# Attention with mixed heads and a SiLU MLP: one maximum instruction for two groups, over two neighbouring PSUM banks

## The chip, the cores and the metric

The kernel runs on one core of one Trainium2 chip. The metric is the device time of one execution in microseconds (us); the median of several executions counts. Engines are called TensorE (PE in the rows, PEld for its weight loads), VectorE (DVE), ScalarE (ACT), GpSimd (POOL) and SyncE (SP, which issues most DMAs).

## What is computed

The attention mixes its 12 heads twice, before and after the softmax; the result goes through a two-layer MLP. All arrays are float32 (the MLP's weights arrive as float64 and are taken apart in the kernel).

```python
# q, k, v: (4, 12, 448, 64); w_pre, w_post: (12, 12)
scores = scale * np.matmul(q, k.transpose(0, 1, 3, 2))
scores = np.einsum('bhij,hg->bgij', scores, w_pre)
scores = scores - np.max(scores, axis=-1, keepdims=True)
attn = np.exp(scores)
attn = attn / (np.sum(attn, axis=-1, keepdims=True) + 1e-09)
attn = np.einsum('bhij,hg->bgij', attn, w_post)
x = np.matmul(attn, v)                # then (tokens 1792, 768)
h = x @ w_in                          # 768 x 2048
out = (h / (1 + np.exp(-h))) @ w_out  # 2048 x 768
```

## The kernel before

The attention is cut into 16 tiles, four to a batch entry, of 100 or 120 query rows each. Within a tile the work runs over **groups** of 10 query rows: 10 rows times 12 heads, padded to 128 partitions, with 448 key columns. Two neighbouring groups are a **pair**; there are 184 groups and 92 pairs. After that comes the MLP (the products of line 624), from about 425 us to the end, in which the change has no instruction.

A pair goes through these steps, and the instruction names below are those of the rows:

- `scores` (lines 339 to 353) computes the scores of a later tile head by head (`pqk`), evicts them to `st` on ScalarE and VectorE, and scatters them by DMA into the rows of `g`.
- `mix_pair` (line 399) is the first head mixing: four products per pair (`pp<-g,wpre`), eight instructions in the trace. They fill two PSUM banks, one for each group. All four are done at about the same time, since two run side by side.
- `top` (line 405) takes the negated maximum of one group's 448 columns into `nm`, on VectorE. A pair needs two such instructions, one behind the other.
- `exp` (line 409) is the exponential on ScalarE, `e<-pp,nm`, with the row sum read out behind it (ACTIVATION_READ_ACCUMULATOR). It reads the group's bank and its `nm`. The first group's exponential is issued in the even step `i`, the second's in the next, odd step; both read PSUM, so the banks are free only after both.
- `bound_sums` and `norm_pair` (lines 418 to 425) make the scaled second mixing weights `wr`.
- `mix_pair_again` (line 437) is the second mixing (`pa<-wr,e`, 64 products per pair), one pair of banks `pa` for all pairs; `put_pair` (line 446) evicts it to `at` on ScalarE, and the next pair's `pa` products wait for that.
- `values` (line 368) multiplies with `v` (`po`), evicted by ScalarE to `x` (line 375).

`LEAD` is 4: the first mixing, maximum and exponentials run two pairs ahead of the second mixing. The order on each engine is the order in which the loop from line 667 writes the instructions; engines run in order. In an even step the loop writes `mix_pair` of the new pair, ScalarE's and VectorE's left-over evictions, the two `top`, and the first `exp`. Beside it the conversion of the MLP's weights (lines 63 to 93, `cw` and `cg`) puts VectorE, ScalarE and GpSimd work between the steps.

PSUM has eight banks: four in pool `ps_m` (scores, transposes, `po`), two in `ps_a` (`pa`, one tile for the whole loop), and two in `ps_p`, two buffers of one bank that every pair takes anew for its two groups. So the first mixing of a pair needs both banks back from the pair before it. During the opening (lines 541 to 556) `ps_p` also serves scores and transposes. The pair of groups 2 and 3 alone takes its banks from `ps_m`.

Of the kernel before, what the change touches and what calls it, by code (L numbers as in the profile page):

```python
# [8 lines left out]
F32 = mybir.dt.float32  # L9
# [4 lines left out]
ALU = mybir.AluOpType  # L14
AX = mybir.AxisListType
PSUM = bass.MemoryType.PSUM
# [87 lines left out]
def talking_heads_then_silu_mlp(  # L104
# [11 lines left out]
    nc = tc.nc  # L116
    ctx.enter_context(tc.manual_schedule())
    B, H, S, D = q.shape
# [4 lines left out]
    GP = 128  # L123
# [41 lines left out]
    mixing = ctx.enter_context(ExitStack())  # L165
    early_p = ctx.enter_context(ExitStack())

    def pool(name, bufs, stack=ctx, **kw):
        return stack.enter_context(tc.tile_pool(name=name, bufs=bufs, **kw))
# [7 lines left out]
    ps_m = pool("ps_m", 4, late_ps, side="right", space=PSUM)  # L177
    e_p = pool("e", 4, mixing, side="right")
    sm = pool("sm", 4, mixing, side="right")
    g_ps = [pool(f"g{o}", 1, st, side="right") for o, st in ((1, mixing), (0, early_p))]  # L180
    ps_p = pool("ps_p", 2, mixing, space=PSUM)
    ps_a = pool("ps_a", 1, mixing, space=PSUM)
    nat = pool("nat", 2, early_p)
    k2_p = pool("k2", 6, early_p)
# [2 lines left out]
    def pair(p, tag, dtype=F32R):  # L187
        return p.tile([128, 2, S], dtype, name=tag, tag=tag)
# [2 lines left out]
    banks = [ps_m]  # L191

    pa = ps_a.tile([128, 2, 512], F32, name="pa", tag="pa")
    turns = []

    def bank(p, name):
        if p is ps_a:
            turns.append(name)
            return pa[:, len(turns) % 2]
        return p.tile([128, 512], F32, name=name, tag="bank")  # L200

    v_tiles = [v2_p.tile([KV, 4, NJ, D], F32, name="v4", tag="v4") for _ in range(4)]
# [61 lines left out]
    def prep_k(b, h):  # L264

        pt = bank(banks[0], "pt")
        kn = kns.pop((b, h))
        for j in range(NJ):
            nc.tensor.transpose(pt[:, j * JT:(j + 1) * JT], kn[:, j].rearrange("p h d -> p (h d)"), ident[:JT, :JT])  # L269

        kh, kl = ks[b, h] = [k2_p.tile([128, S], F32R, name=x, tag=x) for x in ("kh", "kl")]

        def take_high():
            nc.scalar.copy(out=kh, in_=pt[:, :S])

        def take_low():
            nc.vector.tensor_sub(out=kl, in0=pt[:, :S], in1=raw(kh))
        return [(take_high, take_low)]
# [101 lines left out]
    class Group:  # L380
# [12 lines left out]
        def mix_pair(self, other, pool):  # L393

            o, np, p = self.place()
            self.p, other.p = bank(pool, "pp"), bank(pool, "pp")
            for r, c in ((0, 0), (1, 1), (0, 1), (1, 0)):
                rows = slice(HP * r, HP * (r + 1))
                nc.tensor.matmul(  # L399
                    (self, other)[r].p[HP * c:HP * (c + 1), :S], lhsT=wpre[rows],  # L400
                    rhs=gs[self.n][rows, o // R + c * np + p, :], start=True, stop=True)

        def top(self):
            self.nm = sm.tile([GP, 1], F32, name="nm", tag="nm")
            nc.vector.tensor_reduce(out=self.nm, in_=self.p[:GP, :S], axis=AX.X, op=ALU.max, negate=True)  # L405

        def exp(self, sums):
            self.e = e_p.tile([GP, S], F32, name="e", tag="e", bufs=6)
# [52 lines left out]
    at = lambda i: groups[i] if 0 <= i < len(groups) else None  # L461
# [13 lines left out]
    for n in range(1, len(seq)):  # L475
        p0, p1 = first[n - 1], first[n]
        spread = (0, 0, 0, 0, 2, 2) if n == 1 else (-6, -5, -4, -2, -1, 0) if p1 - p0 == 12 else (-6, -5, -4, -3, -2, -1)
        for h in range(0 if n > 1 else 2 * NE, H, 2):
            i = p0 + spread[h // 2]
# [23 lines left out]
    n_last = first[len(seq) - 1]  # L503
# [55 lines left out]
    keep_busy(2)  # L559
    for i in range(0, LEAD, 2):  # L560
        at(i).mix_pair(at(i + 1), (ps_p, ps_m)[i // 2])
        for j in (i, i + 1):
            at(j).top()
        at(i).exp_first()
        at(i + 1).exp(at(i).s[:, 1:2])
        at(i).bound_sums((nc.vector, nc.gpsimd)[i // 2])
        if not i:
            at(0).norm_pair(at(1))
# [29 lines left out]
    def load_part(j):  # L598
        src, k, p = parts[j]
        if src is wo_dram:  # L600
            for _ in conv:
                pass
        raws[j] = box["w"].tile([128, 4, 128], F32R, name="wl", tag="wl", bufs=WB)
        nc.sync.dma_start(out=raw(raws[j]), in_=src[:, 4 * p:4 * p + 4, k])

    def ready_part(j):
        wl = raws.pop(j)
        wh = box["w"].tile([128, 4, 128], F32R, name="wh", tag="wh", bufs=WB)
        nc.scalar.copy(out=wh, in_=raw(wl))  # L609
        nc.gpsimd.tensor_sub(out=wl, in0=raw(wl), in1=raw(wh))  # L610
        ready[j] = wh, wl

    def product(s, p):

        kind, k, u, a = steps[s]
        nk = HC if kind == "i" else HF
        todo = []
        for n in range(nk):
            wh, wl = (x[:, (a * nk + n) % 4] for x in ready[part_of(kind, k, a * nk + n)])
            x = ops[u][n]  # L620
            todo += [(0, wh, x[:, 0]), (1, wh, x[:, 1]), (2, wl, x[:, 0])]
        todo.sort(key=lambda t: t[0])
        for n, (_, w, x) in enumerate(todo):
            nc.tensor.matmul(p[:, :T], lhsT=w, rhs=x, start=(n == 0), stop=(n == len(todo) - 1))  # L624

    def halve(src, dst):

        nc.scalar.copy(out=dst[:, 0], in_=src)
        yield
        nc.vector.tensor_sub(out=dst[:, 1], in0=src, in1=raw(dst[:, 0]))  # L630
# [36 lines left out]
    for i in range(len(groups) + 1):  # L667
        g, new, old = at(i), at(i + LEAD), at(i - 1)
        if i == n_last:
            early_p.close()  # L670
            xw = pool("xw", 1)
            box["w"] = pool("w", 1)

            ops[0] = [pair(xw, f"op0{c}") for c in range(HC)]
            splits = [halve(xs[0][0, 0, c], ops[0][c]) for c in range(HC)]
        for what, args in early[i]:
            what(*args)
        fresh = [new, at(i + LEAD + 1)] if new and i % 2 == 0 else []
        if fresh:
            new.mix_pair(fresh[1], ps_p)  # L680
        if i >= n_last:
            for x in fresh:
                x.top()
        if new and i % 2:
            new.exp(at(i + LEAD - 1).s[:, 1:2])
        for take, _ in done:
            take()
        if 0 < i < len(groups) and i % 2 == 0:
            at(i - 2).put_pair()
        for take, _ in later:  # L690
            if take:
                take()
        if i == len(groups) - 1:
            old.put_pair()
        if any(what is scores for what, _ in work[i]):
            for _, take in later:
                if take:
                    take()
            later = []
        if i < n_last:  # L700
            for x in fresh:
                x.top()
        for _, take in later:
            if take:
                take()
        if i % 2 and at(i + 3):
            at(i + 3).bound_sums()
        if i % 2 == 0 and at(i + 2):
            at(i + 2).norm_pair(at(i + 3))
        if scaled:  # L710
            next(conv)
            scaled = False
        for take in lows:
            take()
        if fresh:
            new.exp_first()
        later, done, highs, lows = [], [], [], []
        for what, args in sorted(work[i], key=lambda x: order.index(x[0])):
            while len(later) + len(done) + len(lows) + 1 + (what is scores) > 4:
                for take in (done or later).pop(0):  # L720
                    if take:
                        take()
            new_takes = what(*args) or []
            if what in (prep_q, prep_k):
                highs += [take for take, _ in new_takes]
                lows += [take for _, take in new_takes]
                new_takes = []
            if what is scores:
                while len(later) > 1:
                    for take in later.pop(0):  # L730
                        if take:
                            take()
            (done if what is values else later).extend(new_takes)
        for take in highs:
            take()
        if i == len(groups) - 2:
            phs.append(bank(ps_m, "ph"))
            product(0, phs[0])
        if g and i % 2 == 0:
            g.mix_pair_again(at(i + 1))  # L740
        if i == len(groups) - 2:
            phs.append(bank(ps_m, "ph"))
            product(1, phs[1])
        if i >= n_last:
            if i >= n_last + 2 and splits:
                if next(splits[0], 1):
                    splits.pop(0)
            if n_last + 2 <= i < n_last + 2 + WB:
                load_part(i - n_last - 2)
        if i in lighter:  # L750
            scaled = next(conv, None)
        if i in (len(groups) - 5, len(groups) - 3):
            ready_part(len(ready))
# [7 lines left out]
    for h in (0, HH):  # L761
        ready_part(len(ready))
        banks[:] = [(ps_m, ps_h)[h // HH]]
        new = values(len(seq) - 1, h // 2, HC)[0]
# [85 lines left out]
    for s, (kind, m, u, a) in enumerate(steps):  # L850
# [14 lines left out]
        p = None  # L865
        if s >= len(phs):
            p = bank(ps_h, "ph")
# [56 lines left out]
```

## Time and profile before

| what | us |
|---|---|
| three executions | 880.78, 886.57, 889.70 |
| their median | 886.57 |
| span of the profiled execution, first to last instruction | 869.5 |
| median less that span | 17.1 |

The profile is of one execution. Its page gives the span alone; what lies around the span is taken from the median, so it is 17.1 us, and 11.3 to 20.2 us by the single executions. Windows and rows give times from the span's start. An engine's busy time is the union of its instructions; a TensorE product that is held back in the middle of a series counts as busy until the series ends.

### The profile page before, as it was taken

The numbers are of one execution on the slowest core, as the hardware profiler recorded it, in microseconds if no ns is written. First come the engines' busy times: TensorE is split into PE (matmuls) and PEld (weight loads), VectorE is DVE, ScalarE is ACT, GpSimd is POOL, SyncE is SP. The second block draws the span as 40 slices with busy tenths as digits, with TensorE's granted clock in tenths as the row PEclk, the third lists the DMA queues.
The fourth block names the chain that finished last, engine by engine and source line by source line (L and its number), as shares of the span: only waits on it lengthen the run. The fifth ranks groups of instructions, "written<-read, shape, count | busy, mean of one in ns | idle before, by whom it ended". The sixth has DMA issues, their size and how long they took to land.

```text
span 869.5 us, 27489 instructions
## 1 busy us (share of the span) xinstructions
PE 825.0 (95%) x11058; PEld 654.1 (75%) x11058; DVE 622.9 (72%) x1218; ACT 526.6 (61%) x1178; POOL 404.4 (47%) x681
## 2 busy tenths in 40 slices
PE   8798999899998999898899999899999999999997
PEld 5355666567665666565799888789999989999886
DVE  5454777577766777666759989998878589983332
ACT  4576888688876878787665652325784346343342
POOL 6131545453645546355856675656642233233020
PEclk8999999999999999999999999999999999999999
DMA  7569778887798877864643553544221142012234
GB/s 148 169 188 207 207 210 242 221 230 211 228 237 220 241 198 216 215 196 139 193 133 125 162 180 104 145 148 140 92 74 49 35 115 81 29 49 73 75 84 106
DMA packets 162343, 132.89 MB, mean 153 GB/s; under 512 B 50409, under 2 KB 155861, under 8 KB 162215
## 3 DMA queue, kind: packets, MB, share of 16 engines
q1 hardware_dynamic: 158809, 129.39, 53.3%
q8 instruction: 87, 1.43, 0.7%
q0 software_dynamic: 544, 1.03, 0.5%
q10 hardware_dynamic: 2862, 0.71, 0.4%
q14 instruction: 41, 0.34, 0.1%
HBM read 64.01 MB, written 27.53 MB: 105 GB/s over the span
## 4 chain that ended last, share of the span: by engine, by line
PE 65%; DVE 15%; DMA 9%; ACT 4%; POOL 3%; issue 3%; SPq 2%; POOLq 0%; DVEq 0%; ACTq 0%
PE ph L624 35%; PE pa L437 8%; PE po L368 7%; PE pp L399 6%; PE pqk L339 6%; DMA g<-st 3%; DVE x L634 2%; DVE op L630 2%; DVE nm L405 2%; DMA qn<-in_q 2%; ACT e L409 2%; DVE cg L92 1%; DMA v<-in_v 1%; PE pt L269 1%; PE ptt L844 1%
## 5 line engine op out<-in xcount | busy, mean ns | idle before, releaser
L624 PE MATMUL ph<-op,wh 128*128 128x448 f32 x924 | 223.5, 370 | 3.7 <-DVE g L823 1.4
L610 POOL TENSOR_TENSOR wl<-wl,wh 128x512 fp32r<-128x512 f32 x84 | 121.3, 1461 | 154.4 <-ACT wh L609 152.0
L624 PEld LDWEIGHTS ph<-op,wh 128*128 128x128 f32 x924 | 172.6, 189 | 20.9 <-DVE g L823 2.7
L405 DVE TENSOR_REDUCE nm<-pp 128x1 f32<-128x448 f32 x184 | 106.1, 618 | 73.1 <-PE pp L399 72.8
L425 POOL TENSOR_SCALAR wr<-wpost,r 128x60 f32<-128x60 f32 x184 | 72.0, 404 | 172.4 <-DVE r L422 120.7
L409 ACT ACTIVATE e<-pp,nm 128x448 f32<-128x448 f32 x184 | 115.4, 631 | 47.9 <-DVE nm L405 45.3
L437 PEld LDWEIGHTS pa<-wr,e 64*64 64x64 f32 (+1 forms) x5888 | 96.0, 131 | 44.3 <-issue 25.8
L437 PE MATMUL pa<-wr,e 64*64 64x60 f32 (+1 forms) x5888 | 108.2, 218 | 14.0 <-ACT at L446 7.7
L624 PE MATMUL ph<-op,wl 128*128 128x448 f32 x462 | 119.6, 367 | 0.4 <-POOL wl L610 0.4
L399 PE MATMUL pp<-g,wpre 64*64 64x448 f32 x736 | 101.9, 573 | 10.8 <-ACT e L409 6.4
L66 POOL TENSOR_TENSOR cg<-cw,cg 128x256 f32<-128x256 f32 x96 | 74.0, 771 | 77.9 <-DVE cw L63 75.7
L624 PEld LDWEIGHTS ph<-op,wl 128*128 128x128 f32 x462 | 87.2, 189 | 7.7 <-POOL wl L610 0.7
L446 ACT COPY at<-pa 120x960 f32<-120x960 f32 x92 | 90.0, 978 | 3.3 <-PE pa L437 3.2
L368 PE MATMUL po<-at,v 120*64 120x120 f32 (+1 forms) x1536 | 87.3, 266 | 2.8 <-issue 2.1
L368 PEld LDWEIGHTS po<-at,v 120*64 120x64 f32 x1536 | 76.4, 138 | 15.2 <-issue 6.4
L90 ACT ACTIVATE cg<-cg,ebias 128x256 int32<-128x256 int32 x96 | 49.6, 516 | 50.8 <-DVE cg L86 49.6
L344 DVE COPY st<-pqk 120x448 f32<-120x448 f32 (+1 forms) x89 | 54.9, 617 | 32.6 <-PE pqk L339 16.8
L609 ACT CAST wh<-wl 128x512 fp32r<-128x512 f32 x84 | 50.9, 617 | 43.1 <-DMA wl<-wo_dram 28.0
L92 DVE SCALAR_TENSOR_TENSOR cg<-cw,cg 128x256 int32<-128x256 int32 x96 | 51.8, 540 | 25.0 <-ACT cg L90 24.7
L624 PE MATMUL ph<-x,wh 128*128 128x448 f32 x252 | 64.8, 365 | 0.0
L339 PEld LDWEIGHTS pqk<-kh,qh 64*120 64x120 f32 (+1 forms) x186 | 18.6, 175 | 43.1 <-issue 14.9
L399 PEld LDWEIGHTS pp<-g,wpre 64*64 64x64 f32 x736 | 23.0, 134 | 37.0 <-ACT e L409 15.5
(122 smaller groups left out, 1398.8 us busy)
## 6 DMA issues: line engine op xcount, KB each, us to landing
g<-st SPq DMA_DIRECT2D x132, 210.0 KB
cw<-in_moe_w_in SPq DMA_DIRECT2D x48, 256.0 KB
cw<-in_moe_w_out SPq DMA_DIRECT2D x48, 256.0 KB
wi_dram<-cg SPq DMA_DIRECT2D x24, 448.0 KB
wo_dram<-cg SPq DMA_DIRECT2D x24, 448.0 KB
wl<-wi_dram SPq DMA_DIRECT2D x42, 256.0 KB
wl<-wo_dram SPq DMA_DIRECT2D x42, 256.0 KB
g<-st SPq DMA_DIRECT2D x48, 175.0 KB
```

The costliest lines, as they stand in the source:

```text
L66: nc.gpsimd.tensor_mul(out=e, in0=m, in1=e)
L92: nc.vector.scalar_tensor_tensor(out=e, in0=hi, scalar=-2 ** 31, in1=e, op0=ALU.bitwise_and, op1=ALU.bitwise_or)
L339: nc.tensor.matmul(ps[i][:m, :S], lhsT=q_[rows, hh, :m], rhs=k_[rows], start=(step == 0), stop=(step == 2))
L368: nc.tensor.matmul(po[i * D:(i + 1) * D, c * m:(c + 1) * m], lhsT=vs[b, h][:, i, j, :], rhs=ats[n][:, j, h + i, :m], start=(j == 0), stop= ...
L399: nc.tensor.matmul((self, other)[r].p[HP * c:HP * (c + 1), :S], lhsT=wpre[rows], rhs=gs[self.n][rows, o // R + c * np + p, :], start=True, ...
L405: nc.vector.tensor_reduce(out=self.nm, in_=self.p[:GP, :S], axis=AX.X, op=ALU.max, negate=True)
L409: nc.scalar.activation(out=self.e, in_=self.p[:GP, :S], func=AF.Exp, bias=self.nm, scale=1.0, accum_out=sums)
L425: nc.gpsimd.tensor_scalar(out=g.wr, in0=wpost.rearrange("p g i -> p (g i)"), scalar1=r[:, i:i + 1], scalar2=1.0, op0=ALU.mult, op1=ALU.mult)
L437: nc.tensor.matmul(half[64 * c:64 * c + m, s, j * GH:(j + 1) * GH], lhsT=g.e[rows, j * JT + c * JH:j * JT + c * JH + m], rhs=g.wr[rows], s ...
L446: nc.scalar.copy(out=ats[self.n].rearrange("p j g t -> p (j g) t")[:, :, o:o + 2 * R].rearrange("p x (c i) -> p x c i", i=RH), in_=pa[:KV] ...
L610: nc.gpsimd.tensor_sub(out=wl, in0=raw(wl), in1=raw(wh))
L624: nc.tensor.matmul(p[:, :T], lhsT=w, rhs=x, start=(n == 0), stop=(n == len(todo) - 1))
```

## The change

The two one-bank buffers of `ps_p` become one tile `pp` of two neighbouring banks that lives through the whole loop; `bank` hands out its halves in turn during the opening. `top` of one group becomes `top_pair` of a pair: one `tensor_reduce` reads `[128, 2, 448]` over both banks and writes two columns of a new tile `nm` `[128, 2]`. The pair from `ps_m` keeps its two instructions. The place of the reductions in the loop is the same.

```diff
-    ps_p = pool("ps_p", 2, mixing, space=PSUM)
+    ps_p = pool("ps_p", 1, mixing, space=PSUM)
...
+    pp = ps_p.tile([128, 2, 512], F32, name="pp", tag="pp")
...
     def bank(p, name):
-        if p is ps_a:
-            turns.append(name)
-            return pa[:, len(turns) % 2]
+        if id(p) in turns:
+            turns[id(p)] += 1
+            return (pa if p is ps_a else pp)[:, turns[id(p)] % 2]
...
-            self.p, other.p = bank(pool, "pp"), bank(pool, "pp")
+            self.p, other.p = (pp[:, 0], pp[:, 1]) if pool is ps_p else (bank(pool, "pp"), bank(pool, "pp"))
...
-        def top(self):
-            self.nm = sm.tile([GP, 1], F32, name="nm", tag="nm")
-            nc.vector.tensor_reduce(out=self.nm, in_=self.p[:GP, :S], axis=AX.X, op=ALU.max, negate=True)
+        def top_pair(self, other, pool):
+            nm = sm.tile([GP, 2], F32, name="nm", tag="nm")
+            self.nm, other.nm = nm[:, 0:1], nm[:, 1:2]
+            if pool is ps_p:
+                nc.vector.tensor_reduce(out=nm, in_=pp[:, :, :S], axis=AX.X, op=ALU.max, negate=True)
+            else:
+                for g in (self, other):
+                    nc.vector.tensor_reduce(out=g.nm, in_=g.p[:GP, :S], axis=AX.X, op=ALU.max, negate=True)
...
-            for x in fresh:
-                x.top()
+        if fresh and i < n_last:
+            new.top_pair(fresh[1], ps_p)
```

On VectorE, in the middle of the loop, one pair's share of the queue before the change (the reductions are line 405; what stands behind them is the reciprocal of an earlier pair and an eviction):

```order
L93 TENSOR_SCALAR cw<-cw 128x256 [waits DVE_49]
L405 TENSOR_REDUCE nm<-pp 128x1 [waits PE_49] x2
L422 RECIPROCAL r<-r 128x2 [waits Pool_49]
L277 TENSOR_TENSOR kl<-pt,kh 128x448 [waits Activation_49]
L86 TENSOR_SCALAR cg<-cw 128x256 [waits DMAHW6_49]
```

The same place of the changed kernel, in which its lines have other numbers (408 is the new reduction):

```order
L93 TENSOR_SCALAR cw<-cw 128x256 [waits DVE_49]
L408 TENSOR_REDUCE nm<-pp 128x2 [waits PE_49]
L428 RECIPROCAL r<-r 128x2 [waits Pool_49]
L278 TENSOR_TENSOR kl<-pt,kh 128x448 [waits Activation_49]
L86 TENSOR_SCALAR cg<-cw 128x256 [waits DMAHW3_49]
```

Two reductions with one column of results each became one with two; the neighbours on the queue are the same.

On TensorE, the first mixing of a pair behind the products with `v`, before the change:

```order
L368 MATMUL po<-at,v_134 64x120 x15
L399 MATMUL pp<-g,wpre 64x448 [waits Activation_49]
L399 MATMUL pp<-g,wpre 64x448 [waits PE_49,Activation_49]
L399 MATMUL pp<-g,wpre 64x448 x2
L339 MATMUL pqk<-kh,qh 120x448 [waits DVE_49] x2
```

The same place of the changed kernel:

```order
L369 MATMUL po<-at,v_135 64x120 x15
L400 MATMUL pp<-g,wpre 64x448 [waits DVE_49,Activation_49]
L400 MATMUL pp<-g,wpre 64x448 x3
L340 MATMUL pqk<-kh,qh 120x448
L340 MATMUL pqk<-kh,qh 120x448 [waits DVE_49]
```

Before, the first product waits for ScalarE's reading of the first bank and the second product for that of the second bank; now the first product carries a wait on ScalarE and VectorE for the tile, and the other three carry none. On no engine does any other instruction change its place.

## Rows read from the trace of the kernel before

**Rows 1.** The page, parts 1 (engines' busy us) and 4 (the chain).
```profile
PE 825.0 (95%) x11058; PEld 654.1 (75%) x11058; DVE 622.9 (72%) x1218; ACT 526.6 (61%) x1178; POOL 404.4 (47%) x681
PE ph L624 35%; PE pa L437 8%; PE po L368 7%; PE pp L399 6%; PE pqk L339 6%; DMA g<-st 3%; DVE x L634 2%; DVE op L630 2%; DVE nm L405 2%; DMA qn<-in_q 2%; ACT e L409 2%; DVE cg L92 1%; DMA v<-in_v 1%; PE pt L269 1%; PE ptt L844 1%
```

**Rows 2.** Windows: length, busy us (instructions) of PE, PEld, DVE, ACT, POOL.
```profile
44.00:425.00 381.00, 357.34 (x8414) 239.07 (x8415) 262.87 (x628) 296.96 (x719) 189.03 (x442) 1.00 0.78 213
```

**Rows 3.** Lines, 0 to 560 us: busy us, mean ns, idle before.
```profile
L405 DVE TENSOR_REDUCE nm<-pp 128x1 f32<-128x448 f32 x184 | 106.1, 618 | 73.1 <-PE pp L399 72.8
L409 ACT ACTIVATE e<-pp,nm 128x448 f32<-128x448 f32 x184 | 115.4, 631 | 47.9 <-DVE nm L405 45.3 <-POOL cg L72 0.7 <-POOL cg L71 0.4
L422 DVE RECIPROCAL r<-r 128x2 f32<-128x2 f32 x92 | 14.4, 157 | 5.0 <-POOL r L418 4.7
L523 DVE MEMSET g<- 128x2688 f32 x1 | 2.3, 2298 | 0.5 <-issue 0.5
```

**Rows 4.** Timeline (start us, length us, instruction) of a pair with spare time.
```profile
121.64 0.98 PE L399 MATMUL pp<-g,wpre 64*64 64x448 f32 x8
122.68 1.16 DVE L405 TENSOR_REDUCE nm<-pp 128x1 f32<-128x448 f32 x2 [0.42 <-PE pp L399]
123.42 0.63 ACT L409 ACTIVATE e<-pp,nm 128x448 f32<-128x448 f32 x1
124.04 0.63 ACT L409 ACTIVATE e<-pp,nm 128x448 f32<-128x448 f32 x1
124.56 0.20 ACT L409 ACTIVATION_READ_ACCUMULATOR e<-pp,nm 128x1 f32 x1
125.25 0.98 PE L399 MATMUL pp<-g,wpre 64*64 64x448 f32 x8
```

**Rows 5.** Timeline, a pair whose products wait for the pair before.
```profile
408.42 1.59 PE L399 MATMUL pp<-g,wpre 64*64 64x448 f32 x8
408.78 0.20 ACT L409 ACTIVATION_READ_ACCUMULATOR e<-pp,nm 128x1 f32 x1
409.03 0.20 PEld L399 LDWEIGHTS pp<-g,wpre 64*64 64x64 f32 x6 [0.43 <-ACT e L409]
410.49 1.14 DVE L405 TENSOR_REDUCE nm<-pp 128x1 f32<-128x448 f32 x2
411.21 0.63 ACT L409 ACTIVATE e<-pp,nm 128x448 f32<-128x448 f32 x1 [0.99 <-DVE nm L405]
```

**Rows 6.** Line 409, 27 to 425 us, who waited for it: us, times.
```profile
  PEld pp L399: 15.5, 25
  PE pp L399: 6.4, 7
```

**Rows 7.** Waits, 44 to 425 us: us in total, times, longest.
```profile
DVE nm L405 <- PE pp L399: 66.3, 68, 4.2
ACT e L409 <- DVE nm L405: 36.1, 54, 2.2
PE pa L437 <- ACT at L446: 6.6, 14, 0.9
```

**Rows 8.** Timeline of TensorE alone, line 399.
```profile
27.92 4.84 PE L399 MATMUL pp<-g,wpre 64*64 64x448 f32 x24 [3.70 <-DMA g<-first]
52.26 1.42 PE L399 MATMUL pp<-g,wpre 64*64 64x448 f32 x8
...
411.99 1.59 PE L399 MATMUL pp<-g,wpre 64*64 64x448 f32 x8 [0.46 <-ACT e L409]
```

**Rows 9.** Timeline at two further places, ScalarE and what follows on TensorE.
```profile
217.97 0.98 ACT L446 COPY at<-pa 120x960 f32<-120x960 f32 x1
219.10 1.11 PE L437 MATMUL pa<-wr,e 64*64 64x60 f32 x63
...
289.89 0.21 ACT L409 ACTIVATION_READ_ACCUMULATOR e<-pp,nm 128x1 f32 x1
290.42 0.98 PE L399 MATMUL pp<-g,wpre 64*64 64x448 f32 x8
```

More of the change, by code (lines that the diff above doesn't have):

```diff
@@ L193, in talking_heads_then_silu_mlp @@
     pa = ps_a.tile([128, 2, 512], F32, name="pa", tag="pa")
-    turns = []
+    pp = ps_p.tile([128, 2, 512], F32, name="pp", tag="pp")
+    turns = {id(ps_a): 0, id(ps_p): 0}
     def bank(p, name):
-        if p is ps_a:
-            turns.append(name)
-            return pa[:, len(turns) % 2]
+        if id(p) in turns:
+            turns[id(p)] += 1
+            return (pa if p is ps_a else pp)[:, turns[id(p)] % 2]
         return p.tile([128, 512], F32, name=name, tag="bank")
@@ L561, in talking_heads_then_silu_mlp @@
         at(i).mix_pair(at(i + 1), (ps_p, ps_m)[i // 2])
-        for j in (i, i + 1):
-            at(j).top()
+        at(i).top_pair(at(i + 1), (ps_p, ps_m)[i // 2])
         at(i).exp_first()
@@ L680, in talking_heads_then_silu_mlp @@
             new.mix_pair(fresh[1], ps_p)
-        if i >= n_last:
-            for x in fresh:
-                x.top()
+        if fresh and i >= n_last:
+            new.top_pair(fresh[1], ps_p)
         if new and i % 2:
@@ L699, in talking_heads_then_silu_mlp @@
             later = []
-        if i < n_last:
-            for x in fresh:
-                x.top()
+        if fresh and i < n_last:
+            new.top_pair(fresh[1], ps_p)
         for _, take in later:
```

## The prediction

> **What bounds the kernel now.** I read the page first [rows 1]: TensorE is busy 95% of the span, and its lines hold 65% of the chain that ended last; the maximum (`nm`) and the exponential (`e`) hold 2% each. So the maximum matters only where TensorE waits for something behind it. The window of the mixing loop comes next [rows 2]: in its 381 us TensorE is busy 357, ScalarE 297 and VectorE 263. VectorE has 118 us to spare there, and 66 of them are waits of the maximum for the first mixing [rows 7]: VectorE isn't what holds the loop. Then the timeline of single pairs shows the ring that the change touches: mixing products, maximum, two exponentials, and back to the products of the next pair, which need both banks.
>
> In a usual pair [rows 4] the products start at 121.64 and the two reductions at 122.68. The first exponential starts at 123.42: 0.74 after the reductions start, 0.12 after the first has ended, while the second still runs. The second exponential starts at 124.04 and its sum is read out by 124.76. TensorE comes to the next pair's products at 125.25, 0.49 after that. Here TensorE had other work, and the ring has time to spare.
>
> In a tight pair [rows 5] the products start at 408.42 on the first bank, but the other weight loads wait until 409.03, which is 0.05 after the read-out of the second exponential (408.78 and 0.20). The series then lasts 1.59 instead of 0.98. There the ring sets the time. In all, 25 weight loads and 7 products waited for line 409 [rows 6]; the timeline of line 399 shows 14 pairs between 44 and 412 us, of which the first and last plain ones stand in [rows 8], that last 1.27 to 1.59 us, and two more start within 0.1 of the read-out. That makes 16 pairs with nothing to spare.
>
> **The change, part by part.**
>
> *The reduction itself.* One of today's takes 618 ns for 448 columns and the reciprocal, an instruction with 2 columns, 157 ns [rows 3]. The difference over 446 columns is 1.03 ns a column; 896 columns then take 157 + 894 x 1.03 = 1.08 us. No row has such an instruction, so it is bounded: above by two of today's with no overlap, 1.24 us; below by 618 ns and 448 columns at the rate of the long memset (2298 ns for 2688 columns, 0.86 ns each [rows 3]), 1.00 us. I take 1.08, from the same operation and memory.
>
> *VectorE's gain.* Two reductions take 1.16 us from start to end [rows 4], so 91 pairs free 91 x 0.08 = 7 us of VectorE (between -7 and 15 by the bounds). I cost this at 0 on the path: the cover is the 66 us that the maximum waits for TensorE anyway [rows 7]. Without the cover it is a gain of 7 us.
>
> The Trainium skill (Perfetto Trace Analysis, Optimizing Scalar/DVE Operations) puts the cost of an instruction's data access on VectorE from PSUM at about 125 ns; by that estimate 91 instructions fewer free 11 us instead of 7, still under the same cover. The same section says that grouping helps when the engine is saturated, and that breaking instructions up may let work end sooner when the engine is not saturated and makes others wait; the window with VectorE busy 263 of 381 us [rows 2] is of the second kind, and so the page speaks against this change.
>
> *The first exponential's start.* It was released at the end of the first reduction, 0.62 after the start, and will be at the end of the only one, 1.08: later by 0.46 us (0.38 to 0.62 by the bounds). The second exponential stands behind it on ScalarE's queue and moves as far. So do the evictions queued behind it (`st`, `at`, `x`, the casts), until ScalarE's next idle stretch takes the delay up. 54 of the first exponentials already waited for the maximum, 36.1 us in all [rows 7]; this should come to roughly 36 + 88 x 0.46 = 76 us.
>
> *What of it reaches TensorE.* I went through the pairs by the time from the read-out of the second exponential to the next products, less the 0.05 us that a release takes:
> - 16 pairs have none to spare: 16 x 0.46 = 7.4 us.
> - 4 pairs have 0.1 to 0.3; the tightest of a second kind is a pair with 0.32 from read-out to products (289.89 and 0.21, then 290.42 [rows 9]). They lose 0.37, 0.36, 0.19 and 0.17: 1.1 us.
> - 19 pairs are like the usual one, with 0.39 to 0.45 to spare [rows 4]: 0.04 each, 0.8 us.
> - The other 50 or so have more than 0.46: nothing.
> - The second mixing waits for the eviction of `pa` 14 times [rows 7]. In most of these ScalarE stood idle ahead of the eviction, for `po`, and takes the delay up there. In two pairs it has no such gap, as at 217.97: the eviction ends at 218.95 and `pa` starts at 219.10 [rows 9]. 2 x 0.45 = 0.9 us.
> - At the loop's opening three pairs' products stand in one series [rows 8]; the third needs the first's banks, so one more delay counts: 0.5 us.
>
> *The wait of the products.* The first product now waits for the whole tile, and before for its own bank. In a tight pair that gave nothing: after the second release at 409.03 the series took another 0.98 us [rows 5], as long as a whole one. Cost 0. If the early start was worth anything, it is at most the 0.61 between 408.42 and 409.03, in 16 pairs 10 us; I keep that for the upper end. What is queued behind the waiting product is TensorE's whole stream, which is why the delays above add up.
>
> The sum: 7.4 + 1.1 + 0.8 + 0.9 + 0.5 = 10.7 us. The profiled span becomes 880.2; with 17.1 around it, as the median has, 897.3 us, against 886.6 before. With a delay of 0.38 the sum is 8 us, with 0.62 it is 17 (16 x 0.62, 4 x 0.43, 19 x 0.2, 1.2 and 0.6).
>
> **The rivals.**
>
> *ScalarE becomes the bound.* ScalarE is idle 84 us in the window [rows 2], 36 of them for the maximum. Of the other 48 the change takes up to 40. Every eviction then comes later than TensorE wants it, and also the pairs with time to spare lose it. Against it: in the usual pair 0.49 us are spare. If half of the 88 x 0.46 reaches TensorE, it is 20 us: 907 us; if all, 40 us: 927.
>
> *It is hidden anyway.* TensorE stands idle 24 us in the window [rows 2] and waits at places that the ring doesn't set, for score scatters and loads. A pair that comes 0.46 later may meet a wait that would have held it all the same. Against it: those waits are fed by the same loop and move with it. Price 0 to 5 us; 889 us.
>
> *Faster.* VectorE's queue behind the maximum (evictions of scores, `cg` and `cw` of the weights) ends earlier by 0.08 us a pair; if that queue, not the exponential, is what TensorE waits for, the gain is 7 us: 879.5, and 15 us or 872 with a reduction of 1.00. It decides only where the maximum starts late because VectorE is behind, as at 410.49 [rows 5]; most starts are set by the products, 68 waits [rows 7]. Over 1% needs a reduction below about 1.06 us and no tight pair at all. The Trainium skill's rule on grouping, in the section named above, would give this if VectorE were saturated.
>
> **How the numbers follow.** The forecast above has a chance of 0.50, with a range of its own from 892 to 905. ScalarE as the bound has 0.17, hidden 0.25, faster 0.08. 1% is 8.9 us, about what a measurement of this kernel, whose runs lie 880.8 to 889.7, can tell from no change. Over 895.4 lie four fifths of the forecast (0.41) and the first rival (0.17): slower 0.58. The rest of the forecast and the hidden case make 0.35 for within 1%, and 0.07 is left for faster. The range from 886 to 911 leaves out the faster case (0.08), the upper half of the first rival (0.08) and the lowest part of the hidden one (about 0.04).
>
> **What the profile after would show.** The reductions: 91 instructions of about 1.08 us; over 1.2 or under 1.0 would make the first term wrong. First exponentials 1.2 us behind the start of the reduction instead of 0.74. ScalarE's waits for the maximum at about 76 us in the window instead of 36. Waits of line 399's loads for line 409 more often than 25 times, and stretched series in some 20 pairs or more. The time from 425 us to the end unchanged. If the loop's end moves by less than 5 us while these waits do appear, the hidden case is right; if it moves by 20, with `at`, `st` and `x` as new causes of TensorE's waits, ScalarE became the bound.

## The result, and the profile after

The changed kernel is slower by 1.28%.

| | before | after |
|---|---|---|
| median of 10 executions, us | 882.5 (874.7 to 889.7) | 891.2 (887.7 to 899.1) |
| ratio, 95% interval | | 1.0128 (1.0086 to 1.0171) |
| span of the profiled execution, us | 869.5 | 886.7 |
| from the last pair's mixing products to the end, us | 451.6 | 451.7 |

The profiled execution after took 888.4 us in all, 1.7 us more than its span. The last line of the table is the span less the end of the last products of line 399 (417.9 us) or of its counterpart, line 400 (435.0 us): behind the loop nothing changed, so all of the difference lies in the loop. The ratio is of undisturbed executions alone: the slowest of before, 889.7 us, lies 1.7% above the fastest and doesn't count in it, so it isn't the quotient of the two medians, 1.0098.

In the changed kernel the first mixing is line 400, the long maximum line 408, the exponential line 415, the reciprocal line 428. First the page's busy times and the window that answers to [rows 2]:

```profile
PE 822.7 (93%) x11058; PEld 653.9 (74%) x11058; DVE 614.4 (69%) x1127; ACT 526.6 (59%) x1178; POOL 403.0 (45%) x681
```

```profile
44.00:434.00 390.00, 351.66 (x8224) 235.16 (x8224) 247.95 (x527) 289.90 (x702) 180.99 (x429) 0.98 0.74 203
```

This window ends just ahead of the last mixing products (435.0 us), that of [rows 2] 7 us behind them (417.9 us), so only the shares compare. VectorE has 8.5 us less to do over the span (622.9 before [rows 1]), and the kernel is longer all the same. By lines, 0 to 560 us, as [rows 3]:

```profile
L415 ACT ACTIVATE e<-pp,nm 128x448 f32<-128x448 f32 x184 | 115.3, 630 | 79.7 <-DVE r L428 63.2 <-DVE nm L408 14.6 <-DVE nm L411 1.0
L408 DVE TENSOR_REDUCE nm<-pp 128x2 f32<-128x896 f32 x91 | 99.2, 1090 | 80.4 <-PE pp L400 78.9 <-ACT st L347 1.1
```

91 reductions of 1.09 us stand where there were 182 of 0.62. ScalarE now stands idle 79.7 us before the exponentials, against 47.9. The profile puts most of that down to the reciprocal (`r`, line 428), which VectorE starts as the maximum ends; the exponential comes 0.1 us behind the maximum's end.

The usual pair of [rows 4], and the wait that now follows it:

```profile
126.37 0.98 PE L400 MATMUL pp<-g,wpre 64*64 64x448 f32 x8
127.49 1.09 DVE L408 TENSOR_REDUCE nm<-pp 128x2 f32<-128x896 f32 x1 [0.41 <-PE pp L400]
128.67 0.63 ACT L415 ACTIVATE e<-pp,nm 128x448 f32<-128x448 f32 x1 [0.50 <-DVE r L428]
129.30 0.63 ACT L415 ACTIVATE e<-pp,nm 128x448 f32<-128x448 f32 x1
129.81 0.20 ACT L415 ACTIVATION_READ_ACCUMULATOR e<-pp,nm 128x1 f32 x1
130.06 0.21 PEld L400 LDWEIGHTS pp<-g,wpre 64*64 64x64 f32 x8 [0.41 <-ACT e L415]
130.07 0.98 PE L400 MATMUL pp<-g,wpre 64*64 64x448 f32 x8
```

Two things come later. The first exponential starts 1.18 us behind the start of the reduction instead of 0.74. And the reduction itself starts 0.14 us behind the end of the products (126.37 and 0.98, then 127.49); before it was 0.05 or 0.06 (121.64 and 0.98, then 122.68 [rows 4]). The next pair's products now wait for the read-out: it ends at 130.01, and they start 0.06 later.

A tight pair, as [rows 5]:

```profile
424.46 0.63 ACT L415 ACTIVATE e<-pp,nm 128x448 f32<-128x448 f32 x1 [0.86 <-DVE r L428]
425.60 0.20 ACT L415 ACTIVATION_READ_ACCUMULATOR e<-pp,nm 128x1 f32 x1
425.85 0.98 PE L400 MATMUL pp<-g,wpre 64*64 64x448 f32 x8 [0.95 <-ACT e L415]
```

Here TensorE stood idle for 0.95 us until the exponential let the banks go. Who waited for line 415, 27 to 442 us, as [rows 6]:

```profile
  PEld pp L400: 31.7, 44
  PE pp L400: 16.9, 16
```

25 weight loads had waited 15.5 us and 7 products 6.4 us; now it is 44 loads and 31.7 us, 16 products and 16.9 us.

### The profile page after: what moved, and what is told of

Same layout as the page of the kernel before. It is cut to its first block, busy times and chain, and to the rows that moved or that the text cites. A ratio compares the mean times of both kernels' runs of the same rounds, so it can differ in the third digit from the quotient of the medians.

```text
span 886.7 us, 27443 instructions
## 1 busy us (share of the span) xinstructions
PE 822.7 (93%) x11058; PEld 653.9 (74%) x11058; DVE 614.4 (69%) x1127; ACT 526.6 (59%) x1178; POOL 403.0 (45%) x681
## 4 chain that ended last, share of the span: by engine, by line
PE 60%; DVE 15%; DMA 8%; ACT 6%; issue 5%; SPq 3%; POOL 2%; DVEq 0%; ACTq 0%; POOLq 0%
PE ph L629 34%; PE po L369 6%; PE pa L443 6%; PE pp L400 6%; DMA g<-st 5%; PE pqk L340 5%; ACT e L415 3%; DVE nm L408 2%; DVE op L635 2%; DVE x L639 2%; SPq L250 2%; DVE cg L92 2%; DVE cw L93 1%; PE ptt L847 1%; ACT at L452 1%
## 5 line engine op out<-in xcount | busy, mean ns | idle before, releaser
L415 ACT ACTIVATE e<-pp,nm 128x448 f32<-128x448 f32 x184 | 115.3, 630 | 79.7 <-DVE r L428 63.2
L408 DVE TENSOR_REDUCE nm<-pp 128x2 f32<-128x896 f32 x91 | 99.2, 1090 | 80.4 <-PE pp L400 78.9
L443 PEld LDWEIGHTS pa<-wr,e 64*64 64x64 f32 (+1 forms) x5888 | 98.7, 133 | 48.9 <-issue 32.1
L443 PE MATMUL pa<-wr,e 64*64 64x60 f32 (+1 forms) x5888 | 111.3, 221 | 16.9 <-ACT at L452 8.0
L400 PE MATMUL pp<-g,wpre 64*64 64x448 f32 x736 | 92.4, 573 | 21.5 <-ACT e L415 16.9
L92 DVE SCALAR_TENSOR_TENSOR cg<-cw,cg 128x256 int32<-128x256 int32 x96 | 50.0, 521 | 36.7 <-ACT cg L90 36.6
L340 PE MATMUL pqk<-kh,qh 64*120 64x448 f32 (+1 forms) x184 | 47.4, 461 | 6.4 <-ACT st L347 4.7
```

The costliest lines, as they stand in the source:

```text
L92: nc.vector.scalar_tensor_tensor(out=e, in0=hi, scalar=-2 ** 31, in1=e, op0=ALU.bitwise_and, op1=ALU.bitwise_or)
L340: nc.tensor.matmul(ps[i][:m, :S], lhsT=q_[rows, hh, :m], rhs=k_[rows], start=(step == 0), stop=(step == 2))
L400: nc.tensor.matmul((self, other)[r].p[HP * c:HP * (c + 1), :S], lhsT=wpre[rows], rhs=gs[self.n][rows, o // R + c * np + p, :], start=True, ...
L408: nc.vector.tensor_reduce(out=nm, in_=pp[:, :, :S], axis=AX.X, op=ALU.max, negate=True)
L415: nc.scalar.activation(out=self.e, in_=self.p[:GP, :S], func=AF.Exp, bias=self.nm, scale=1.0, accum_out=sums)
L443: nc.tensor.matmul(half[64 * c:64 * c + m, s, j * GH:(j + 1) * GH], lhsT=g.e[rows, j * JT + c * JH:j * JT + c * JH + m], rhs=g.wr[rows], s ...
```

## Experiments

Three theories stood at the start. **A**: the first exponential is held until the end of the one long maximum; this reaches TensorE where the ring from the mixing products over the maximum and both exponentials back to the products has no time to spare. **B**: the one tile over two banks costs the time, since its first product waits for both banks and its maximum has one more wait. **C**: ScalarE's queue as a whole is full, and any delay on it is lost time. Each ratio below is against the kernel before, run in turn on the same chip.

| run | first exponential behind the products' end, us | ratio (95% interval) |
|---|---|---|
| before | 0.78 | 1 |
| changed kernel | 1.32 | 1.0128 (1.0086 to 1.0171) |
| e1, one tile, two maxima | 1.41 | 1.0139 (1.0077 to 1.0200) |
| e2, two tiles, second maximum first | 1.36 | 1.0123 (1.0073 to 1.0172) |
| e3, one tile, one maximum of half the columns | 0.86 | 1.0020 (0.9982 to 1.0058) |
| e4, a new tile for each pair | 1.28 | 1.0129 (1.0089 to 1.0170) |
| e5, as e1 with two `nm` tiles | 1.41 | 1.0177 (1.0126 to 1.0228) |
| e9, before with half the columns | 0.56 | 0.9919 (0.9884 to 0.9954) |
| e10, changed kernel with a further reduction | 1.87 | 1.0356 (1.0312 to 1.0400) |

The second column is the median over the pairs from the seventh on of the time from the products' end to the maximum's start, plus that from there to the first exponential; for e10 the start is that of the further reduction.

**e1: one tile, two maxima again.**

```diff
-            if pool is ps_p:
-                nc.vector.tensor_reduce(out=nm, in_=pp[:, :, :S], axis=AX.X, op=ALU.max, negate=True)
-            else:
-                for g in (self, other):
-                    nc.vector.tensor_reduce(out=g.nm, in_=g.p[:GP, :S], axis=AX.X, op=ALU.max, negate=True)
+            for g in (self, other):
+                nc.vector.tensor_reduce(out=g.nm, in_=g.p[:GP, :S], axis=AX.X, op=ALU.max, negate=True)
```

> The one tile over two banks of the changed kernel, with its waits, but again two maximum instructions, one a bank. Theory A (the first exponential is held until the end of the one long reduction, 0.47 us later, and this reaches TensorE where the ring of a pair has no time to spare): the first exponential is back at about 0.72 us behind the start of the reductions, and the time is that of before within 0.5%, ratio 1.000 to 1.005 (the reduction still starts 0.14 instead of 0.05 us behind the products, which costs some 2 to 3 us in the tight pairs). Theory B (the cost lies in the one tile: the first product waits for both banks, the reduction has one more wait): as the changed kernel, 1.010 to 1.016.

Measured: 1.0139. That looks like B, but the premise of the expectation did not hold: the first exponential did not come back. Its timeline:

```profile
132.48 1.16 DVE L408 TENSOR_REDUCE nm<-pp 128x1 f32<-128x448 f32 x2 [0.53 <-PE pp L400]
133.75 0.63 ACT L412 ACTIVATE e<-pp,nm 128x448 f32<-128x448 f32 x1 [0.73 <-DVE r L425]
```

The two maxima end at 133.64 and the first exponential follows at 133.75, behind both. The run has both the one tile and the delay, and tells nothing apart.

**e2: the delay without the one tile.** In the kernel before, the loop's two maxima change places.

```diff
-            for x in fresh:
+            for x in fresh[::-1]:
                 x.top()
...
```

The same edit stands at the second place where the loop writes the maxima.

> The kernel before with two tiles, only that in the loop the second group's maximum is taken ahead of the first group's, so that the first exponential is released at the end of both, about 1.28 us behind the start instead of 0.72. No tile and no count of instructions changes. Theory A: slower as the changed kernel or slightly more, 1.010 to 1.018, and TensorE's waits for the exponential go from 25 to some 40. Theory B: the time of before, 0.997 to 1.003. Theory C (the delay matters because ScalarE's queue as a whole is full): also slower, so this run doesn't tell A from C.

Measured: 1.0123. Timeline and waits (44 to 440 us):

```profile
131.22 1.16 DVE L405 TENSOR_REDUCE nm<-pp 128x1 f32<-128x448 f32 x2 [0.43 <-PE pp L399]
132.49 0.64 ACT L409 ACTIVATE e<-pp,nm 128x448 f32<-128x448 f32 x1 [0.67 <-DVE r L422]
```

```profile
PEld pp L399 <- ACT e L409: 22.2, 41, 3.6
```

The exponential starts 1.27 us behind the start of the maxima, and 41 loads wait for it. Tiles, banks and the number of instructions are those of before; the later first exponential alone costs as much as the whole change. This is A's clearest run.

**e3: the one tile and the one instruction without the delay.**

```diff
-                nc.vector.tensor_reduce(out=nm, in_=pp[:, :, :S], axis=AX.X, op=ALU.max, negate=True)
+                nc.vector.tensor_reduce(out=nm, in_=pp[:, :, :S // 2], axis=AX.X, op=ALU.max, negate=True)
```

> The changed kernel, with the maximum taken over the first 224 of the 448 columns of each group (the shift of the softmax is then not the row's maximum). One instruction over two banks as in the changed kernel, but it should take about 0.62 us (157 ns + 446 x 1.03 ns) instead of 1.09. Theory A: the first exponential starts 0.72 us behind the start of the reduction as before, and the loss is gone: 0.998 to 1.004. Theory B: 1.010 to 1.016 as the changed kernel.

Measured: 1.0020, no difference. Timeline and waits:

```profile
131.92 0.62 DVE L408 TENSOR_REDUCE nm<-pp 128x2 f32<-128x448 f32 x1 [0.35 <-PE pp L400]
132.64 0.64 ACT L415 ACTIVATE e<-pp,nm 128x448 f32<-128x448 f32 x1 [0.55 <-DVE r L428]
```

```profile
PEld pp L400 <- ACT e L415: 14.3, 21, 3.9
```

With the exponential back at 0.72 us the loads wait 21 times again. B falls as the main cause: the one tile with its waits costs 0.6% at the most (the interval's end), if the halved maxima gain nothing else. VectorE had some 43 us less to do in this run (56.7 us of maxima by its lines, against 99.2), and the run is no faster than before; e9 below, which halves the maxima without the one tile, gains some 3 us more than A accounts for, and a gain of that size could hide as much of the tile's cost here.

**e4: the maximum's additional wait taken away.** Every pair takes a new two-bank tile, so the maximum waits for the products alone.

```diff
-            self.p, other.p = (pp[:, 0], pp[:, 1]) if pool is ps_p else (bank(pool, "pp"), bank(pool, "pp"))
+            if pool is ps_p:
+                self.pp = ps_p.tile([128, 2, 512], F32, name="pp", tag="pp")
+                self.p, other.p = self.pp[:, 0], self.pp[:, 1]
+            else:
+                self.p, other.p = bank(pool, "pp"), bank(pool, "pp")
...
-                nc.vector.tensor_reduce(out=nm, in_=pp[:, :, :S], axis=AX.X, op=ALU.max, negate=True)
+                nc.vector.tensor_reduce(out=nm, in_=self.pp[:, :, :S], axis=AX.X, op=ALU.max, negate=True)
```

> The changed kernel with its one long maximum, but every pair takes a new two-bank tile from the pool, so that the reduction again waits for the products alone and should start 0.05 instead of 0.14 us behind them. Theory A: the delay of the first exponential falls from 0.56 to 0.47 us, a sixth less: 1.009 to 1.013 where the changed kernel has 1.013. Theory B, as far as the reduction's additional wait is meant: back near before, 1.000 to 1.004.

Measured: 1.0129. The start moved as intended; the products end at 130.87 and the maximum follows 0.07 behind:

```profile
129.89 0.98 PE L404 MATMUL pp<-g,wpre 64*64 64x448 f32 x8
130.94 1.09 DVE L412 TENSOR_REDUCE nm<-pp 128x2 f32<-128x896 f32 x1 [0.40 <-PE pp L404]
```

A gain of a sixth of the loss, 0.2%, is less than this measurement can tell. Only that the additional wait isn't the main cause is shown.

**e5: e1 with an `nm` tile for each group.** The diff is against e1.

```diff
-            nm = sm.tile([GP, 2], F32, name="nm", tag="nm")
-            self.nm, other.nm = nm[:, 0:1], nm[:, 1:2]
             for g in (self, other):
+                g.nm = sm.tile([GP, 1], F32, name="nm", tag="nm")
                 nc.vector.tensor_reduce(out=g.nm, in_=g.p[:GP, :S], axis=AX.X, op=ALU.max, negate=True)
```

> The one tile over two banks of the changed kernel and its waits, but two maximum instructions that write two tiles nm, one for each group, as in the kernel before. Theory A (the later first exponential costs the time): the first exponential starts 0.72 us behind the start of the reductions, the ratio is 1.000 to 1.005. Theory B (the one tile costs it): 1.010 to 1.016.

Measured: 1.0177, and again the premise failed:

```profile
134.08 1.16 DVE L407 TENSOR_REDUCE nm<-pp 128x1 f32<-128x448 f32 x2 [0.54 <-PE pp L400]
135.35 0.64 ACT L411 ACTIVATE e<-pp,nm 128x448 f32<-128x448 f32 x1 [0.72 <-DVE r L424]
```

The exponential reads its own bank and its own `nm`, and still starts behind both maxima (135.24); so it does, by 0.11 to 0.12 us, in every pair from the seventh on. The one tile is all that is left to set it there. That an order between VectorE's and ScalarE's readings holds for the whole tile and not for the bank fits this, but isn't shown. It answers B in another way: the one tile does cost time with two maxima, but its first exponential, at 1.41 us, is also as late as that of e2 (1.36), which has two tiles and loses 1.2%.

**e6 and e7: is ScalarE full?** The changed kernel and the kernel before, both without the activation of the weights' conversion.

```diff
-        nc.scalar.activation(out=e, in_=e, func=AF.Relu, scale=8.0, bias=ebias)
```

> The changed kernel without the activation of line 90 (96 x 0.52 us of ScalarE's work in the conversion of the MLP's weights; the weights are then not converted rightly). Theory C (ScalarE's queue is full, and that is why a later exponential costs time): against the same edit of the kernel before, run beside it, the loss shrinks to under 0.4%. Theory A (the ring from the products over the maximum and the two exponentials back to the products, which holds no such activation in most tight pairs): the loss stays at 1 to 1.5% of the time.

> The kernel before without the activation of line 90 (the weights are then not converted rightly). The base for the run beside it. Theory A: within 1% of before, since TensorE isn't held by ScalarE's load in most pairs: 0.990 to 1.000. Theory C: also near before, with all the gain in the changed kernel.

Measured: 1.0125 (1.0069 to 1.0181) for e6, 1.0016 (0.9979 to 1.0053) for e7. With 50 us less on ScalarE the loss is still there: 1.1% by the two ratios, 1.4% by the medians (890.9 against 878.8 us). The waits, first e6, then e7:

```profile
PEld pp L399 <- ACT e L414: 30.3, 40, 3.4
```

```profile
PEld pp L398 <- ACT e L408: 9.7, 18, 2.0
```

C falls: it is not ScalarE's load that makes the delay count.

**e8: the first group's products first.**

```diff
-            for r, c in ((0, 0), (1, 1), (0, 1), (1, 0)):
+            for r, c in ((0, 0), (0, 1), (1, 1), (1, 0)):
```

> The kernel before with the four mixing products of a pair in the order first group, first group, second, second, so that in a tight pair the first group's two products run as soon as its bank is free, and its maximum starts about 0.6 us earlier. Theory A: in a row of tight pairs (49 to 65, 236 to 246 and 400 to 417 us) the ring gets shorter by up to 0.6 us each; 4 to 8 such pairs give 2 to 5 us: 0.994 to 0.999. If the products of one group don't run side by side with the other's in this order, every pair takes up to 0.9 us more of TensorE: 1.05 or more.

Measured: 1.0002 (0.9959 to 1.0046). No cost of the order can be told, and where the ring is tight the maximum does start ahead of the series' end (56.25):

```profile
54.85 1.40 PE L399 MATMUL pp<-g,wpre 64*64 64x448 f32 x7
55.89 1.16 DVE L405 TENSOR_REDUCE nm<-pp 128x1 f32<-128x448 f32 x2 [0.97 <-PE pp L399]
```

A cost of 0.9 us in every pair, 1.05, is ruled out; the expected gain of 2 to 5 us is inside the interval. Inconclusive.

**e9: an earlier first exponential.** The kernel before with both maxima over half the columns.

```diff
-            nc.vector.tensor_reduce(out=self.nm, in_=self.p[:GP, :S], axis=AX.X, op=ALU.max, negate=True)
+            nc.vector.tensor_reduce(out=self.nm, in_=self.p[:GP, :S // 2], axis=AX.X, op=ALU.max, negate=True)
```

> The kernel before with its two maximum instructions, each over the first 224 of the 448 columns (the shift of the softmax is then not the row's maximum). The first exponential should start about 0.5 instead of 0.72 us behind the start of the reductions. Theory A: only the 16 pairs with no time to spare gain, 16 x 0.23 = 3.7 us: 0.993 to 1.000. If every pair's delay counted, 92 x 0.23 = 21 us: 0.976.

Measured: 0.9919, a gain of 7 us where A had 3.7. Each maximum takes 385 ns (by lines, 0 to 560 us), and 7 loads wait for an exponential (44 to 440 us):

```profile
L405 DVE TENSOR_REDUCE nm<-pp 128x1 f32<-128x224 f32 x184 | 63.1, 385 | 78.8 <-PE pp L399 78.6
```

```profile
PEld pp L399 <- ACT e L409: 3.8, 7, 1.2
```

The direction is A's, but the size is just outside what was expected: 0.42% stands outside the interval of 0.5 to 1.2%. In its profile the small steps (last table) come to -4.0 us, which is A's size; what the other 3 us of the medians are, the runs don't settle. It is no version to keep, since a maximum over half a row doesn't bound the exponentials of the other half.

**e10: the delay doubled.** The changed kernel with one more reduction ahead of the long one.

```diff
+                more = sm.tile([GP, 1], F32, name="more", tag="more")
+                nc.vector.tensor_reduce(out=more, in_=pp[:, 0, :S], axis=AX.X, op=ALU.max, negate=True)
                 nc.vector.tensor_reduce(out=nm, in_=pp[:, :, :S], axis=AX.X, op=ALU.max, negate=True)
```

> The changed kernel with one more reduction over one bank (its result is not used) ahead of the long one, so that the first exponential is released another 0.54 us later, 1.1 us later than in the kernel before in all. Theory A, by the same list of pairs and their spare times in the trace of before: 58 to 62 pairs lose time, 36 to 42 us: 1.035 to 1.048, more than twice the loss of the changed kernel, since pairs that had 0.5 to 1.0 us to spare now lose too. If the loss grew in proportion to the delay: 1.025.

Measured: 1.0356, 31 us, clearly above the 1.025 of a loss in proportion and at the low end of A's range of ratios. But the expectation's own 36 to 42 us are 1.041 to 1.048 of before, and the 31 us lie under them: the list of spare times promised more than came.

```profile
133.55 0.62 DVE L409 TENSOR_REDUCE more<-pp 128x1 f32<-128x448 f32 x1 [0.30 <-ACT at L454]
134.09 1.08 DVE L410 TENSOR_REDUCE nm<-pp 128x2 f32<-128x896 f32 x1
```

```profile
PEld pp L400 <- ACT e L417: 51.5, 53, 2.8
PE pp L400 <- ACT e L417: 36.9, 44, 2.7
```

The second half of the delay costs more (20 us) than the first (11 us): as A has it, it finds pairs whose spare time the first half has used up.

**e11 and e12: both kernels profiled once more.**

> The kernel before, unchanged, profiled once more: is its first profile a fast execution? Compared pair by pair with the first profile (start of the products of line 399), all steps between neighbouring pairs of at most 0.8 us together should come to 0 within 2 us, and the larger steps, which are waits for DMA at the change of tiles, to about +7 to +11 us, as they do in e3, e7 and e8. If the larger steps come to less than 3 us, part of the 17 us between the two first profiles is the change's after all.

> The changed kernel, unchanged, profiled once more. Theory A: against the first profile of before the steps of at most 0.8 us come to +9 to +12 us again, with the larger steps between +4 and +13 us, whatever these are in this execution.

The two first profiles differ by 17.2 us, the medians by 8.7 and the ratio by 11. To see what the rest is, I took the ends of the first-mixing products pair by pair, from the seventh pair to the last, and added up by how much each interval differs from the first profile of before: steps of up to 0.8 us apart from larger ones. I set that limit after having seen the first profiles; with any limit from 0.6 to 1.2 us the changed kernel's two profiles have 9 to 15 us in small steps, and e11, e3, e7 and e8 at most 1.3.

| profile against the first one of before | small steps, us | larger steps, us (their number) |
|---|---|---|
| before again (e11) | +1.3 | +4.7 (8) |
| e3, e7, e8 (no later exponential) | +0.3, +0.1, -2.6 | +10.9, +8.4, +10.7 (7 to 11) |
| changed kernel | +10.1 | +7.0 (11) |
| changed kernel again (e12) | +11.2 | +7.4 (11) |
| e1, e2, e5 | +13.2, +13.6, +12.1 | +7.4, +7.2, +6.5 (7 to 12) |
| e4, e6 | +8.5, +8.5 | +13.5 (17), +10.6 (12) |
| e9 | -4.0 | +7.5 (10) |
| e10 | +18.7 | +16.6 (22) |

The small steps split the kernels as the theory does; in e10, where a tight pair loses 1.1 us, the limit no longer sorts. The expectations of e11 and e12 speak of the starts of the products, not of their ends. By the starts the changed kernel has +1.5 in small and +15.7 in larger steps, and e12 +4.8 and +13.8, so e12's expectation failed as it was worded. A held series of before starts once its first bank is free, one of the changed kernel only at the second release, up to 0.61 us later [rows 5], and that carries steps over the limit; e2, which keeps two tiles, has +14.0 and +6.9 by the starts too.

The larger steps appear in every profile, with or without the change, mostly at the change of tiles; for the kernel before itself they were 4.7 us, less than expected. So the first profile of before was one of its shortest executions, and some 5 to 7 of the 17 us belong to that.

One rival was left: TensorE's granted clock. It was 0.989 of full speed in the first profile of before (span 869.5 us) and 0.990 in e12 (887.3 us); the changed kernel is longer at the same clock. The larger steps do go with it. The profiles at 0.980 or less (e3, e4, e6, e8) have 10.6 to 13.5 us of them, the others, e10 apart, 4.7 to 8.4.

## Why the prediction was right, step by step

- **The direction, the place and the mechanism** hold. Later exponentials reach TensorE through the tight pairs; e2 gives the whole loss without the new tile, e3 takes the loss away with it. The predicted ratio was 897.3/886.6 = 1.012, the measured one 1.0128.
- **The length of the reduction**: 1.08 from the rate of two rows; measured 1.09.
- **The first exponential**: 0.46 us later behind the start of the reduction; measured 0.74 to 1.18, which is 0.44, and 0.46 by the medians over the pairs.
- **VectorE's gain at 0**: right. VectorE's busy time fell by 8.5 us (7 forecast), and e3, which frees 43 us more, is no faster than before; e9's open 3 us leave a doubt of that size. The Trainium skill (Perfetto Trace Analysis, Optimizing Scalar/DVE Operations) says that breaking instructions up may let work end sooner where their engine is not saturated but makes others wait; VectorE busy 248 of 390 us and a slower kernel agree with it. The estimate of 11 us freed, worked out from its figure, is above the 8.5 measured.
- **The wait of the products, cost 0**: the tight pair agrees, the products start 0.05 us behind the read-out before and after. The 10 us kept for the upper end weren't needed: e3 has that wait and no loss clear of noise.
- **A step that was missing**: the reduction starts 0.14 us behind the products instead of 0.05. In the changed kernel's trace 67 of the 93 reductions carry a wait for ScalarE, against 36 of 184 before; the place of the queue shown ahead of the prediction is one without. The delay was then 0.54 us, not 0.46, and the 19 pairs with 0.39 to 0.45 to spare lose 0.09 to 0.15 each, about 2.4 us instead of 0.8. From the seventh pair on the same list of pairs gives 9.2 us with 0.46 and 12.3 with 0.54, and 10.1 and 11.2 were traced: a part was taken up elsewhere. So the close agreement of the sum is in part luck: a delay taken too small made up for a list that promises too much. In e4 only 4 reductions carry that wait, and they start 0.07 us behind the products; its price stays below what can be measured.
- **What lies around the span**: wrong. I took 17.1 us from the median; the execution after has 1.7 (888.4 less 886.7), and so has before in e11 (877.07 less 875.3). Its first profile thus belongs to an execution of about 871 us, shorter than all ten that were timed, and I read it as a usual one. The predicted time isn't touched by that, since the sum was added to the median of three. It lies 6.1 us above the measured 891.2: 4.1 of them because ten executions have the median 882.5 where three had 886.6, the other 2.0 because the sum was 10.7 and the medians differ by 8.7. As a time, 891.2 lies just under the forecast's own range of 892 to 905 and under the 895.4 set for 1%; it is the ratio that was met.
- **Signs that were to show**: ScalarE's waits at 76 us came to 70 (44 to 440 us, 63.2 put down to the reciprocal and 6.5 to the maximum). Loads waiting more than 25 times came to 44. That series would be stretched in 20 pairs or more was wrong in form: since the first product now carries the wait, TensorE's wait stands ahead of the series, and from the seventh pair on only 3 series last over 1.2 us, against 14.
- **The rivals**: that ScalarE becomes the bound falls with e6 and e7. Its sign was a loop's end 20 us later with `st`, `at` and `x` as new causes; the end moved by 17.1 us in the first two profiles, by 12.3 from e11 to e12, and TensorE's waits for `st` and `at` in the scores and the first mixing add up to 22 us in both first profiles (44 to 440 us). That it is hidden anyway falls with the interval. Faster by VectorE's queue falls with the loss itself.
- **Slips that change nothing**: of the 14 longer series one lasts 2.38 us (at 262.83), not 1.59 at the most; and four fifths of 0.50 is 0.40, not 0.41, so the chances for slower add up to 0.57.

- **The second mixing's wait for the eviction**, 0.9 us in the sum, doesn't show: 14 waits of 6.0 us now, 14 of 6.6 before [rows 7].

Three rows of waits of the changed kernel, 44 to 440 us, carry the figures of 70 and 6.0:

```profile
ACT e L415 <- DVE r L428: 63.2, 76, 2.0
ACT e L415 <- DVE nm L408: 6.5, 9, 1.3
PE pa L443 <- ACT at L452: 6.0, 14, 0.8
```

## What to carry to other kernels

One long instruction for two consumers gives the first consumer its result only at the end: before two are joined, look for who waits for the first, and how much time is spare on the way from there back to the engine that bounds the kernel. The busy time saved on an engine that isn't the bound gained nothing that could be told here; the delay costs in every round whose spare time is smaller than it, so a list of spare times, round by round, foretells the loss, here to within a third (12.3 us against 10.1 and 11.2 traced; 36 to 42 against 31 for twice the delay). And one tile over two PSUM banks can hold back the reader of the first bank until both are done with, even with two instructions (e1, e5).

## What the runs showed that was not expected

- With one tile, the first exponential stood behind the maxima of both banks, although it needs one (e1, e5: 0.11 us behind the end of both). The runs show the order and the price of these kernels, 1.4 to 1.8%; whether the hardware would need it was not tried.
- The four mixing products of a pair may be written in either order at no cost that shows (e8, 1.0002, at most 0.5%).
- Executions of the kernel before lie between 872 and 895 us, and they go with TensorE's granted clock: of the 23 beside e5 to e8, the five at 0.989 or more took 871.9 to 875.4 us, the four at 0.979 or less 880.4 to 886.7. The loop differs at the change of tiles, where evictions wait for the scatter of scores to land. The same eviction waited 0.87 us in the first profile of before and 1.40 us in e11, first and second fence:

```profile
83.60 0.62 DVE L344 COPY st<-pqk 100x448 f32<-100x448 f32 x1 [0.87 <-DMA g<-st]
84.25 0.98 PE L399 MATMUL pp<-g,wpre 64*64 64x448 f32 x8
```

```profile
84.49 0.62 DVE L344 COPY st<-pqk 100x448 f32<-100x448 f32 x1 [1.40 <-DMA g<-st]
85.73 1.77 PE L399 MATMUL pp<-g,wpre 64*64 64x448 f32 x8
```

Ahead of the scores' products at this place TensorE stood idle for 1.47 us in the first profile and for 2.67 in e11, both until an eviction on ScalarE:

```profile
83.48 0.44 PE L339 MATMUL pqk<-kh,qh 64*100 64x448 f32 x1 [1.47 <-ACT st L346]
```

```profile
84.36 0.69 PE L339 MATMUL pqk<-kh,qh 64*100 64x448 f32 x1 [2.67 <-ACT st L346]
```

Behind the longer idle time the granted clock stood at 0.50, the level of 1.2 GHz, and in the first profile at 1.00, the level of 2.4 GHz (the number ahead of the last two in these windows, first profile and e11):

```profile
83.30:86.70 3.40, 3.22 (x37) 1.65 (x41) 2.27 (x6) 2.15 (x6) 0.74 (x1) 1.00 0.74 217
```

```profile
84.40:87.80 3.40, 3.40 (x15) 1.32 (x16) 2.03 (x5) 2.03 (x5) 0.74 (x1) 0.50 0.82 231
```

In this stretch the mixing products took 1.77 instead of 0.98 us. Such steps make the difference of two single profiles larger or smaller than that of the medians, and only the comparison pair by pair told them from the change.
